# Strassen's algorithm for the up-projection of two chunks at a time, with weight sums kept in DRAM

## The chip, the cores and the metric

The kernel runs on one core of one Trainium2 chip. The metric is the device time of one execution in microseconds. A core has five engines that run side by side, each through its own queue in order: TensorE (PE in the profile, with its weight loads as PEld), VectorE (DVE), ScalarE (ACT), GpSimd (POOL), and SyncE (SP), which here only issues DMAs. PSUM, where matmuls accumulate, has eight banks of 512 float32 per partition.

## The reference

Sliding-window attention (8 batches, 8 heads, 576 positions, head dimension 64) is followed by a feed-forward part over all 4608 tokens:

```python
    scores = scale * np.matmul(q, k.transpose(0, 1, 3, 2))
    mask = (rel >= 0) & (rel < window)          # window = 128
    scores = np.where(mask, scores + bias[None], -1000000000.0)
    ...
    attn = attn / (np.sum(attn, axis=-1, keepdims=True) + 1e-09)
    return np.matmul(attn, v).astype(np.float32)
...
    h = x @ w_in                                # x 4608 x 512, w_in 512 x 2048
    g = h * (1.0 / (1.0 + np.exp(-1.702 * h)))
    return (g @ w_out).astype(np.float32)       # w_out 2048 x 512
```

x is the attention's output with the heads side by side. All data are float32.

## The kernel before

**Precision.** TensorE multiplies in a rounded 32-bit type (fp32r). Each operand is therefore kept as a high part, its rounded copy, and a low part, the difference; a product is three matmuls: high by high, low by high, high by low. The high part is a cast or copy on ACT or DVE, the low part a subtraction on POOL or DVE.

**Feed-forward.** The tokens are 18 chunks of T = 256; the 2048 hidden columns are 16 blocks f of 128 columns. For one chunk and one f, `Job.up` (L548) multiplies x (transposed, four blocks k of 128 rows) by the block of w_in: 12 matmuls of 128x256 (L552) into one PSUM tile `h_ps`. GELU is Tanh on ACT (L557) and one DVE operation (L558); `gh` (L561, ACT) and `gl` (L562, POOL) are its parts. `Job.down` (L565) multiplies them by the block of w_out: three terms by two row blocks, 6 matmuls of 512 columns (L571) into `acc0` and `acc1`, which stay open over all 16 f. A factor of two in GELU is taken out at the end (L587), and the result is sent from ACT's queue. `split_x` (L532) makes the parts of a chunk's x when the chunk begins. The two weights are decoded once into SBUF tiles `w1_0` to `w1_15` and `w2_0` to `w2_15`, each with both parts, and stay there.

**Attention.** It is software-pipelined: one `tick` (L609) takes one unit one step further. The first two batches are 24 units of another kind, all done early; each of the other six batches is 20 units (120 in all), of two blocks of 128 queries, or one at the end of a head pair. A unit's steps are: loads from SP's queue (`load`, `load_v`, kept in program order by `move`), splits, scores on PE (L334, PSUM tile `s_ps`, one bank), bias and row minimum on DVE (L362), Exp on ACT (L381), division on DVE, transposes on PE (L442, PSUM tile `t_ps`, two banks), high part on ACT (L455), low part on DVE (L461), product with V on PE (L499, `x_ps`), and sums into the chunk's x (`xf`, four buffers). PSUM's eight banks are `s_ps` 1, `t_ps` 2, `x_ps` 1, `h_ps` 2, `acc0`, `acc1`.

**Order.** The program goes through steps (chunk, f). In each step it first lets as many ticks go as the batches' due times ask for (L701 to L710), then issues `up` of the next step, then `down` of this one:

```python
        credit += pace
        while credit >= 1 and ticks < last:
            credit -= 1
            tick()
        ...
                j.up(nf)
        ...
        j.down(f)
```

A batch must be done two steps and a bit ahead of the first chunk that reads it (`SLACK`), and may start only when a chunk far enough along has begun (`start`, `seen`), since `xf` has four buffers. From chunk 2 on, one batch falls on two chunks, apart from chunk 6 and chunks 15 to 17, which have next to none.

This is not yet the order on the engines. The program is built with `schedule_with_timeline_sim=True`: a planner simulates the engines and gives each its queue, taking what is ready by its own times, the earlier in the program first. PSUM and SBUF tiles are handed out in the same simulation; a tile with a `tag` shares the buffers of that tag. `keep_in_program_order` and `in_turn` fix parts of the order. What the planner has ordered is carried out strictly, with semaphore waits.

Of the kernel before, what the change touches and what calls it, by code (L numbers as in the profile page):

```python
# [8 lines left out]
F32 = mybir.dt.float32  # L9
F32R = mybir.dt.float32r  # L10
# [3 lines left out]
AF = mybir.ActivationFunctionType  # L14
# [6 lines left out]
P = 128  # L21
# [23 lines left out]
SPINS = 10, 6, 6, 6, 6, 6, 6  # L45

# [96 lines left out]
def tile_kernel(ctx: ExitStack, tc: tile.TileContext, q0, k0, v0, qT, kT, v, w_in, w_out, out):  # L143
# [7 lines left out]
    ps = ctx.enter_context(tc.tile_pool(name="ps", bufs=1, space=PSUM))  # L151

# [276 lines left out]
    def flip(u):  # L429
# [4 lines left out]
        u.t = ps.tile([P, 4 * P], F32, name="t_ps", bufs=2)  # L434
# [28 lines left out]
    open_x = {}  # L463

# [67 lines left out]
    def split_x(c, x):  # L532
        xh = xp.tile([P, NC, T], F32R, name="xh")
        xl = xp.tile([P, NC, T], F32R, name="xl")
        for k in range(NC):
            (nc.scalar.copy if c in BESIDE else nc.vector.tensor_copy)(xh[:, k], x[:, k])
            sub = nc.vector if k % 2 else nc.gpsimd
            sub.tensor_tensor(xl[:, k], x[:, k], xh[:, k].bitcast(F32), ALU.subtract)
        return xh, xl

    class Job:


        def __init__(self, c, f0, f1, begun=None):
            self.c, self.f0, self.f1, self.begun = c, f0, f1, begun
            self.gs = {}

        def up(self, f):  # L548
            h = ps.tile([P, T], F32, name="h_ps", bufs=2)
            ops = [(z, x, k) for z, x in ((0, self.xh), (1, self.xh), (0, self.xl)) for k in range(NC)]  # L550
            for n, (z, x, k) in enumerate(ops):
                nc.tensor.matmul(  # L552
                    h, w1[f][:, z, k * P:(k + 1) * P], x[:, k],
                    start=(n == 0), stop=(n == len(ops) - 1))
# [20 lines left out]
        def finish(self):  # L575
# [6 lines left out]
            for t, acc in enumerate(self.acc):  # L582
# [6 lines left out]
                nc.scalar.dma_start(out[at:at + P, :], o[:, t])  # L589

# [81 lines left out]
    jobs += [Job(c, 0, NF) for c in range(2, NCH)]  # L672
    starts = {}
    steps = 0
    for j in jobs:
        starts.setdefault(j.c, steps)
        steps += j.f1 - j.f0
    now, credit, first_x = 0, 0.0, xf[0]
# [4 lines left out]
    def begin(j):  # L683
        j.xh, j.xl = split_x(j.c, xf.pop(j.c, first_x))
        j.up(j.f0)

    begin(jobs[0])
    seen = 0
    flat = [(j, f) for j in jobs for f in range(j.f0, j.f1)]
    for now, (j, f) in enumerate(flat):  # L690
# [10 lines left out]
        pace, last = 0.0, 0  # L701
        for n, by, start in due:
            if start > seen:
                break
            last = n + 3
            pace = max(pace, (n + 3 - ticks - credit) / max(starts[by] - 1 - SLACK - now, 1))
        credit += pace
        while credit >= 1 and ticks < last:
            credit -= 1
            tick()  # L710
# [7 lines left out]
        j.down(f)  # L718
        if f == j.f1 - 1:
            j.finish()  # L720
# [53 lines left out]
```

## Time and profile before

| | us |
|---|---|
| median of 3 runs | 1064.84 (1064.75 to 1067.0) |
| the profiled execution's own time | 1068.36 |
| its span, first to last instruction | 1066.3 |
| PE busy / weight loads | 1052.9 / 929.1 |
| DVE / ACT / POOL busy | 660.5 / 597.2 / 603.5 |
| DMA | 78.45 MB, 74 GB/s over the span |
| mean granted TensorE clock | 0.995 |

A matmul's busy time contains its way through the pipeline, so that neighbours overlap; starts of successive matmuls give the pace. In rows of instructions, the text is: line, engine, operation, output <- inputs, shape, count, then busy time and mean duration of one in ns, then idle time of the engine before them and what ended it. Rows with a time first are from the timeline: start, duration, engine, line.

### The profile page before, as it was taken

Reading aid. Unit: us, or ns where it says so; the run is one execution under the profiler, and the core shown is the slowest. Engines: PE = TensorE matmul, PEld = TensorE weight load, DVE = VectorE, ACT = ScalarE, POOL = GpSimd, SP = SyncE. Lnnn points to the kernel's source line nnn. Section 1 sums busy time; section 2 is a strip of 40 time slices with the busy share of each in tenths; the row PEclk is TensorE's granted clock in tenths of the full one; section 3 lists DMA queues with packets and bytes.
Section 4 is the critical chain, followed back from the end, with each engine's and each line's share of the span. In section 5 each row is a group of like instructions: output and inputs, shape, how many; then the busy total and the mean of one; then the engine's idle time right before and its main releaser. Section 6 shows DMA issues by size and latency. Waiting matters only on the chain.

```text
span 1066.3 us, 21362 instructions
## 1 busy us (share of the span) xinstructions
PE 1052.9 (99%) x7041; PEld 929.1 (87%) x7041; DVE 660.5 (62%) x2117; ACT 597.2 (56%) x1811; POOL 603.5 (57%) x863
## 2 busy tenths in 40 slices
PE   9899999999999999999999999999999999999998
PEld 5567787889989999999999999999999999998987
DVE  6797522568887777545767668767877687313121
ACT  6879853466666565535555556655665656322222
POOL 4579933567676666554656557656666665323232
PEclk9899999999999999999999999999999999999999
DMA  8872001223222132102121223212222221000000
GB/s 307 281 261 73 25 22 56 73 67 96 75 76 81 51 102 67 57 14 71 54 79 52 71 62 91 66 60 78 79 63 85 57 78 28 20 2 20 1 21 20
DMA packets 88109, 78.45 MB, mean 74 GB/s; under 512 B 36800, under 2 KB 79296, under 8 KB 88000
## 3 DMA queue, kind: packets, MB, share of 16 engines
q1 hardware_dynamic: 82240, 67.14, 21.4%
q10 hardware_dynamic: 5760, 9.96, 2.6%
q8 instruction: 55, 0.90, 0.3%
q14 instruction: 54, 0.44, 0.1%
HBM read 67.63 MB, written 9.44 MB: 72 GB/s over the span
## 4 chain that ended last, share of the span: by engine, by line
PE 94%; DVE 3%; ACT 1%; DMA 1%; issue 1%; POOL 0%; SPq 0%; DVEq 0%; POOLq 0%; ACTq 0%
PE h_ps L552 38%; PE acc L571 37%; PE s_ps L334 5%; PE x_ps L499 5%; PE t_ps L442 4%; PE x_ps L476 2%; PE t_ps L419 1%; PE sb_ps L324 1%; PE s_ps L324 1%; DVE wc L213 1%; DMA rw<-w_out 1%; ACT pb L374 1%; DVE rec L392 0%; PE acc L189 0%; DVE rw L212 0%
## 5 line engine op out<-in xcount | busy, mean ns | idle before, releaser
L562 POOL TENSOR_TENSOR gl<-g,gh 128x256 fp32r<-128x256 f32 x288 | 218.0, 757 | 292.2 <-ACT gh L561 224.9
L552 PE MATMUL h_ps<-xh,w 128*128 128x256 f32 x2304 | 370.2, 284 | 1.1 <-POOL w L217 0.6
L552 PEld LDWEIGHTS h_ps<-xh,w 128*128 128x128 f32 x2304 | 328.5, 189 | 34.5 <-issue 2.8
L571 PE MATMUL acc<-w,gh 128*128 128x512 f32 x1152 | 324.9, 400 | 0.0
L558 DVE SCALAR_TENSOR_TENSOR g<-g,h_ps 128x256 f32<-128x256 f32 x288 | 119.6, 415 | 207.9 <-ACT g L557 206.5
L557 ACT ACTIVATE g<-h_ps 128x256 f32<-128x256 f32 x288 | 110.4, 383 | 229.4 <-PE h_ps L552 207.3
L571 PEld LDWEIGHTS acc<-w,gh 128*128 128x128 f32 x1152 | 196.5, 189 | 27.9 <-ACT g L557 0.3
L552 PE MATMUL h_ps<-xl,w 128*128 128x256 f32 x1152 | 194.6, 280 | 0.0
L561 ACT CAST gh<-g 128x256 fp32r<-128x256 f32 x288 | 116.9, 406 | 129.5 <-DVE g L558 121.1
L571 PE MATMUL acc<-w,gl 128*128 128x512 f32 x576 | 188.0, 401 | 0.0
L552 PEld LDWEIGHTS h_ps<-xl,w 128*128 128x128 f32 x1152 | 164.2, 188 | 6.0
L312 POOL TENSOR_TENSOR K<-rk,K 128x384 fp32r<-128x384 f32 (+1 forms) x120 | 109.0, 909 | 65.2 <-ACT Q L292 15.9
L381 ACT ACTIVATE pb<-pb,mins 128x256 f32<-128x256 f32 (+2 forms) x216 | 104.9, 487 | 43.8 <-DVE mins L362 40.1
L571 PEld LDWEIGHTS acc<-w,gl 128*128 128x128 f32 x576 | 92.6, 188 | 9.5 <-issue 0.9
L311 POOL TENSOR_TENSOR Q<-rq,Q 64x256 fp32r<-64x256 f32 (+1 forms) x120 | 83.1, 692 | 22.2 <-DVE K L310 4.9
L406 DVE TENSOR_SCALAR pb<-pb,rec 128x256 f32<-128x256 f32 (+2 forms) x216 | 91.8, 461 | 3.2
L362 DVE CUSTOM_DVE_ANT_0 pb<-s_ps,bias 128x256 f32<-128x256 f32 (+3 forms) x240 | 85.7, 377 | 4.1 <-PE s_ps L334 2.8
L392 DVE TENSOR_SCALAR rec<-sums 128x2 f32<-128x2 f32 (+3 forms) x144 | 48.5, 336 | 58.4 <-ACT pb L381 53.6
L334 PE MATMUL s_ps<-K,Q 128*128 128x256 f32 (+1 forms) x432 | 79.8, 289 | 0.4 <-DVE mins L362 0.4
L310 DVE CAST K<-rk 128x384 fp32r<-128x384 f32 (+1 forms) x120 | 52.5, 438 | 41.2 <-PE s_ps L334 34.2
L461 DVE TENSOR_TENSOR pl<-t_ps,ph 128x512 fp32r<-128x512 f32 (+2 forms) x120 | 72.2, 604 | 9.3 <-ACT ph L455 6.6
L442 PE MATMUL t_ps<-ident,pb 128*128 128x128 f32 x408 | 74.2, 272 | 0.0
(68 smaller groups left out, 1322.2 us busy)
## 6 DMA issues: line engine op xcount, KB each, us to landing
rk<-kT SPq DMA_DIRECT2D x72, 192.0 KB, 2.5
rq<-qT SPq DMA_DIRECT2D x96, 128.0 KB, 2.3
out<-o ACTq DMA_DIRECT2D x36, 256.0 KB, 2.1
rw<-w_in SPq DMA_DIRECT2D x16, 512.0 KB, 6.5
rw<-w_out SPq DMA_DIRECT2D x16, 512.0 KB, 7.0
rk<-kT SPq DMA_DIRECT2D x48, 128.0 KB, 2.2
rv<-v SPq DMA_DIRECT2D x96, 64.0 KB, 1.9
rq<-q SPq DMA_DIRECT2D x16, 128.0 KB, 2.6
```

The source lines that it names most:

```text
L312: nc.gpsimd.tensor_tensor(K2, rk, K1.bitcast(F32), ALU.subtract)
L334: nc.tensor.matmul(u.s[:b.rows, e, b.first:b.end], u.Q[:, b.q0 - u.q0:b.q0 - u.q0 + b.rows], k[:, ko:ko + b.end - b.first], start=(z == 0) ...
L362: nc.vector.tensor_tensor_reduce(b.p[ra:rb, cs:b.end], u.s[ra:rb, e, cs:b.end], bias[head][ra:rb, cs:b.end], -SCALE, BIG, ALU.add, ALU.min ...
L381: nc.scalar.activation(live, live, AF.Exp, bias=u.mins[:b.rows, e:e + 1], scale=-1.0, accum_out=u.sums[:b.rows, e:e + 1],)
L406: nc.vector.tensor_scalar(live, live, u.rec[:rows, e:e + 1], None, ALU.mult)
L442: nc.tensor.transpose(u.t[:c.n, w:w + b.rows], b.p[:b.rows, col:col + c.n], ident[:b.rows, :b.rows])
L552: nc.tensor.matmul(h, w1[f][:, z, k * P:(k + 1) * P], x[:, k], start=(n == 0), stop=(n == len(ops) - 1))
L557: nc.scalar.activation(g, h, AF.Tanh, scale=0.851)
L558: nc.vector.scalar_tensor_tensor(g, g, 1.0, h, ALU.add, ALU.mult)
L561: nc.scalar.copy(gh, g)
L562: nc.gpsimd.tensor_tensor(gl, g, gh.bitcast(F32), ALU.subtract)
L571: nc.tensor.matmul(acc, g[:, t * P:(t + 1) * P], w2[f][:, z], start=(f == self.f0 and n == 0), stop=(f == self.f1 - 1 and n == 2))
```

## The change

Chunks 0 to 3 stay as they are. From chunk 4 on (`S0`) two chunks and two blocks f are one step of a 2 x 2 block product: the halves of the 512 rows of w_in are the block rows, the two f the block columns, and the two chunks the columns of x. Strassen's algorithm in Winograd's form makes the four results from seven block products instead of eight. Each product is 6 matmuls of 128x256 (two k, three terms). The results come together in two PSUM tiles, X and Y: products are added to X while copies of its state between them go to SBUF, and DVE adds Y. Two of the four results are read by GELU from SBUF, in a tile of 512 columns for both chunks.

- **Weight sums** (`sums`): from step 33 (chunk 2) to chunk 4, for each pair of f, POOL and DVE form four sums of blocks, ACT and POOL split them, and they and three plain blocks are written to DRAM from SP's queue, seven factors of 256 KB for each of eight pairs of f.
- **Ring** (`factor`): the factors come back two at a time, 512 KB, from SP's queue, into a ring of five tiles, in the place of `w1_7` to `w1_11`; a tile is asked for four tiles ahead.
- **Operands** (`Pair.split`): the seven sums of x are formed in place and split into seven tiles in the place of `w1_0` to `w1_6`, one buffer each.
- **GELU's parts** (`keep`): four tiles in the place of `w1_12` to `w1_15`.
- **Down-projection**: four accumulators for the two chunks, in `acc0`, `acc1` and the two banks of `h_ps`; it runs one pair of f behind, in quarters of six matmuls between the products.
- **PSUM of the attention**: X and Y take the two banks of `t_ps`; the transposes share the one bank of `s_ps`.
- **Due times**: a batch is due by the first chunk of the pair that reads it; the steps of a pair are 32 quarters.

```diff
+S0 = 4
+T2 = 2 * T
+RING = 5
+SUMS_FROM = 33
+ORDER = "A11", "A12", "S2", "S3", "S1", "S4", "A22"
+OPERANDS = "B11", "B21", "T2", "T3", "T1", "B22", "T4"
...
+    dram = ctx.enter_context(tc.tile_pool(name="dram", bufs=1, space=bass.MemoryType.DRAM))
...
-        u.t = ps.tile([P, 4 * P], F32, name="t_ps", bufs=2)
+        u.t = ps.tile([P, 4 * P], F32, name="t_ps", tag="s_ps" if paired else "t_ps", bufs=1 if paired else 2)
...
+    def sums(j):
+        f, g = w1[2 * j], w1[2 * j + 1]
+        H = 2 * P
+        for name, src in (("A11", f[:, :, :H]), ("A12", f[:, :, H:]), ("A22", g[:, :, H:])):
+            nc.sync.dma_start(part(j, name), src.bitcast(F32))
+        a = ffn.tile([P, 2 * H], F32, name="sa", tag="o", bufs=3)
+        b = ffn.tile([P, 2 * H], F32, name="sb", tag="o", bufs=3)
+        nc.gpsimd.tensor_tensor(a, g[:, 0].bitcast(F32), g[:, 1].bitcast(F32), ALU.add)
+        nc.gpsimd.tensor_tensor(b, f[:, 0].bitcast(F32), f[:, 1].bitcast(F32), ALU.add)
+        nc.vector.tensor_tensor(a[:, H:], a[:, :H], a[:, H:], ALU.add)
...
+        for s, names in ((a, ("S3", "S1")), (b, ("S2", "S4"))):
+            st = xp.tile([P, 2, 2 * H], F32R, name="st", tag="x0")
+            nc.scalar.copy(st[:, 0], s)
+            nc.gpsimd.tensor_tensor(st[:, 1], s, st[:, 0].bitcast(F32), ALU.subtract)
+            for i, name in enumerate(names):
+                nc.sync.dma_start(part(j, name), st[:, :, i * H:(i + 1) * H].bitcast(F32))
...
+    def factor(n):
+        tile_, side = divmod(n, 2)
+        while len(ring) < min(tile_ + RING, (NCH - S0) // 2 * len(parts)):
+            r = const.tile([P, 2, 2, 2 * P], F32R, name="ring", tag=f"w1_{len(OPERANDS) + len(ring) % RING}")
+            nc.sync.dma_start(r.bitcast(F32), parts[len(ring) % len(parts)])
+            ring.append(r)
+        return ring[tile_][:, side]
...
+            def cut(name, src):
+                i = OPERANDS.index(name)
+                t = self.x[name] = const.tile([P, 2, 2, T], F32R, name="x" + name, tag=f"w1_{i}")
+                nc.scalar.copy(t[:, 0], src)
+                on = nc.vector if i % 2 else nc.gpsimd
+                on.tensor_tensor(t[:, 1], src, t[:, 0].bitcast(F32), ALU.subtract)
+            cut("B11", a1)
+            cut("B21", a2)
+            nc.vector.tensor_tensor(a1, b1, a1, ALU.subtract)
+            cut("B22", b2)
+            nc.vector.tensor_tensor(b1, b2, b1, ALU.subtract)
+            nc.vector.tensor_tensor(b2, b2, a1, ALU.subtract)
+            cut("T2", b2)
+            cut("T3", b1)
+            cut("T1", a1)
+            nc.vector.tensor_tensor(a2, a2, b2, ALU.subtract)
+            cut("T4", a2)
...
+        def up(self, j, q):
+            if q == 0:
+                self.X = ps.tile([P, T], F32, name="X_ps", tag="t_ps", bufs=2)
+                self.product(j, 0, self.X, True)
+                self.p = ffn.tile([P, T], F32, name="p", tag="g")
+                nc.scalar.copy(self.p, self.X)
+                self.Y = ps.tile([P, T], F32, name="Y_ps", tag="t_ps", bufs=2)
+                self.product(j, 1, self.Y, True)
+                nc.vector.tensor_tensor(self.p, self.Y, self.p, ALU.add)
+                self.g = xp.tile([P, T2], F32, name="g1", tag="xh1")
+                self.gelu(self.g[:, :T], self.p)
+            elif q == 1:
+                self.product(j, 2, self.X, False)
+                self.u = xp.tile([P, T2], F32, name="u", tag="xh0")
+                nc.scalar.copy(self.u[:, :T], self.X)
+            elif q == 2:
+                self.product(j, 3, self.Y, True)
+                self.product(j, 4, self.X, False)
+                nc.scalar.copy(self.u[:, T:], self.X)
+                nc.vector.tensor_tensor(self.u[:, T:], self.Y, self.u[:, T:], ALU.add)
+            else:
+                self.product(j, 5, self.X, False)
+                self.gelu(self.g[:, T:], self.X)
+                self.keep(2 * j, self.g)
+                self.product(j, 6, self.Y, False)
+                nc.vector.tensor_tensor(self.u[:, :T], self.Y, self.u[:, :T], ALU.add)
+                g = xp.tile([P, T2], F32, name="g2", tag="xl0")
+                self.gelu(g, self.u)
+                self.keep(2 * j + 1, g)
+        def down(self, j, q):
+            if j == 0 and q == 0:
+                self.acc = [ps.tile([P, DM], F32, name="accs", tag=tag, bufs=bufs)
+                            for tag, bufs in (("acc0", 1), ("acc1", 1), ("h_ps", 2), ("h_ps", 2))]
+            f = 2 * j + q // 2
...
+        if now >= SUMS_FROM and made < NF // 2 and (now - SUMS_FROM) * NF // 2 >= made * (len(flat) - SUMS_FROM):
+            sums(made)
+            made += 1
...
+    paired = True
+    before = None
+    for c in range(S0, NCH, 2):
+        pair = Pair(c)
+        pair.split()
+        seen = c + 1
+        for i in range(NF // 2 * 4):
+            now += 1
+            advance(now)
+            pair.up(i // 4, i % 4)
...
+            elif i < 4:
+                before.down(NF // 2 - 1, i)
+            else:
+                pair.down(i // 4 - 1, i % 4)
+        before = pair
```

More of the change, by code (lines that the diff above doesn't have):

```diff
@@ L463, in tile_kernel @@
     open_x = {}
+    paired = False
     def mix_whole(u):
@@ L552, in up @@
                 nc.tensor.matmul(
-                    h, w1[f][:, z, k * P:(k + 1) * P], x[:, k],
+                    h, w1[f][:, z, k * P:(k + 1) * P], x[k],
                     start=(n == 0), stop=(n == len(ops) - 1))
@@ L671, in tile_kernel @@
     jobs.append(Job(0, F0, NF, jobs[0]))
-    jobs += [Job(c, 0, NF) for c in range(2, NCH)]
+    jobs += [Job(c, 0, NF) for c in range(2, S0)]
     starts = {}
@@ L677, in tile_kernel @@
         steps += j.f1 - j.f0
+    for c in range(S0, NCH):
+        starts[c] = steps + (c - S0) // 2 * 2 * NF
     now, credit, first_x = 0, 0.0, xf[0]
@@ L685, in begin, with advance @@
         j.up(j.f0)
+    def advance(now):
+        nonlocal credit
+        pace, last = 0.0, 0
+        for n, by, start in due:
+            if start > seen:
+                break
+            last = n + 3
+            pace = max(pace, (n + 3 - ticks - credit) / max(starts[by] - 1 - SLACK - now, 1))
+        credit += pace
+        while credit >= 1 and ticks < last:
+            credit -= 1
+            tick()
     begin(jobs[0])
-    seen = 0
+    seen, made = 0, 0
     flat = [(j, f) for j in jobs for f in range(j.f0, j.f1)]
@@ L699, in tile_kernel @@
                 decode_next()
[L701 to L710, printed above, removed]
+        advance(now)
+        if now >= SUMS_FROM and made < NF // 2 and (now - SUMS_FROM) * NF // 2 >= made * (len(flat) - SUMS_FROM):
+            sums(made)
+            made += 1
         if now + 1 < len(flat):
@@ L717, in tile_kernel @@
                 seen = max(seen, nj.c)
-        j.down(f)
-        if f == j.f1 - 1:
-            j.finish()
+            j.down(f)
+            if f == j.f1 - 1:
+                j.finish()
+    while made < NF // 2:
+        sums(made)
+        made += 1
+    paired = True
[6 more added lines that the diff above has]
+            now += 1
+            advance(now)
+            pair.up(i // 4, i % 4)
+            if before is None:
+                if i == 1:
+                    j.down(f)
+                    j.finish()
+                if i >= 4:
+                    pair.down(i // 4 - 1, i % 4)
+            elif i < 4:
+                before.down(NF // 2 - 1, i)
+            else:
+                pair.down(i // 4 - 1, i % 4)
+        before = pair
+    for q in range(4):
+        before.down(NF // 2 - 1, q)
 def build(nc, arrays):
```

62 lines of the change are left out of this document (58 added, 4 removed).

## The prediction

> **What bounds the kernel now.** I read the page first, then busy time by stretches of two chunks, then the order of the last matmuls.
>
> ```profile
> span 1066.3 us, 21362 instructions
> PE 1052.9 (99%) x7041; PEld 929.1 (87%) x7041; DVE 660.5 (62%) x2117; ACT 597.2 (56%) x1811; POOL 603.5 (57%) x863
> ...
> GB/s 307 281 261 73 25 22 56 73 67 96 75 76 81 51 102 67 57 14 71 54 79 52 71 62 91 66 60 78 79 63 85 57 78 28 20 2 20 1 21 20
> ```
>
> ```profile
> 0.00:45.00 45.00, 40.26 (x239) 25.47 (x239) 29.97 (x117) 31.85 (x99) 20.07 (x30) 0.93 0.81 274
> 90.00:130.00 40.00, 40.00 (x257) 31.07 (x257) 24.36 (x67) 38.95 (x113) 37.44 (x34) 1.00 0.15 42
> ...
> 186.10:307.30 121.20, 121.20 (x840) 108.75 (x839) 88.26 (x294) 76.62 (x244) 78.11 (x119) 1.00 0.28 78
> 307.30:424.10 116.80, 116.37 (x803) 106.93 (x803) 89.41 (x302) 70.71 (x219) 76.81 (x120) 1.00 0.27 75
> ...
> 581.60:697.10 115.50, 115.50 (x797) 106.55 (x796) 82.33 (x282) 68.36 (x209) 73.47 (x113) 1.00 0.25 70
> ...
> 923.70:1012.40 88.70, 88.70 (x574) 80.21 (x573) 21.28 (x48) 25.14 (x64) 26.75 (x36) 1.00 0.04 13
> ```
>
> The columns after the length are PE, PEld, DVE, ACT and POOL busy, granted clock, DMA share, GB/s. PE is never idle from chunk 2 (begun at 186.1) to the last chunk but for 0.4 us in one stretch; DVE is at most 77% busy (89.4 of 116.8). Two chunks beside a batch of attention take 115.5 us, two chunks alone 88.7 us. So the kernel is PE's queue, and a change is worth the matmuls that it takes out less the idle time that it makes. Busy time counts a matmul's pipeline, so the price of one is read from starts:
>
> ```profile
> 1054.62 1.09 PE L571 MATMUL acc<-w,gh 128*128 128x512 f32 x4
> 1055.55 0.28 PE L552 MATMUL h_ps<-xl,w 128*128 128x256 f32 x1
> 1055.67 0.63 PE L571 MATMUL acc<-w,gl 128*128 128x512 f32 x2
> 1056.14 1.10 PE L552 MATMUL h_ps<-xh,w 128*128 128x256 f32 x8
> 1057.08 0.62 PE L552 MATMUL h_ps<-xl,w 128*128 128x256 f32 x4
> 1057.54 1.09 PE L571 MATMUL acc<-w,gh 128*128 128x512 f32 x4
> 1058.47 0.63 PE L571 MATMUL acc<-w,gl 128*128 128x512 f32 x2
> 1058.94 1.09 PE L571 MATMUL acc<-w,gh 128*128 128x512 f32 x4
> ```
>
> Twelve up-matmuls of 256 columns go from 1056.14 to 1057.54, 116.7 ns each; six down-matmuls of 512 columns from 1057.54 to 1058.94, 233 ns each. Two chunks of 192 and 96 would be 89.6 us; the stretch shows 88.7. The single L552 at 1055.55, between two pieces of L571, shows that the planner mixes work of two steps.
>
> **What is removed.** Before, two chunks and two f take 4 groups of 12 up-matmuls, 48. After, seven products of 6 (two k, three high/low terms), 42, of the same 128x256 shape. Seven pairs of chunks by eight pairs of f by 6 is 336 matmuls, at 116.7 ns **39.2 us**. The down-projection keeps its 12 matmuls for each f and chunk pair (four row blocks, three terms), attention keeps all of its own. Nothing is added to PE. A pair falls to 115.5 − 5.6 = 109.9 us beside attention and to 83.1 us alone.
>
> **What is added beside PE.** The durations:
>
> ```profile
> L558 DVE SCALAR_TENSOR_TENSOR g<-g,h_ps 128x256 f32<-128x256 f32 x288 | 119.6, 415 | 207.9 <-ACT g L557 206.5
> L557 ACT ACTIVATE g<-h_ps 128x256 f32<-128x256 f32 x288 | 110.4, 383 | 229.4 <-PE h_ps L552 207.3
> L561 ACT CAST gh<-g 128x256 fp32r<-128x256 f32 x288 | 116.9, 406 | 129.5 <-DVE g L558 121.1 <-PE acc L571 5.6 <-DVE rec L393 1.4
> ...
> L217 POOL TENSOR_TENSOR w<-wc,w 128x512 fp32r<-128x512 f32 x32 | 45.9, 1442 | 6.6 <-ACT w L216 6.4
> ...
> L587 DVE TENSOR_SCALAR o<-acc 128x512 f32<-128x512 f32 x34 | 22.2, 684 | 6.0 <-PE acc L571 6.0
> ...
> L216 ACT CAST w<-wc 128x512 fp32r<-128x512 f32 x32 | 20.2, 630 | 4.8 <-DVE wc L213 4.6
> ...
> L584 DVE TENSOR_TENSOR o<-acc,xf 128x512 f32<-128x512 f32 x2 | 1.3, 686 | 0.4 <-DMA rv<-v 0.4
> ```
>
> ```profile
> L538 DVE TENSOR_TENSOR xl<-xf,xh x10: 412/928/958, 582.8 to 814.7; 128x256 fp32r<-128x256 f32 x10
> L538 POOL TENSOR_TENSOR xl<-xf,xh x10: 782/787/923, 583.1 to 813.1; 128x256 fp32r<-128x256 f32 x10
> ```
>
> DVE, for each pair of f: three adds and the GELU multiply that read PSUM, 4 × 0.415; one GELU multiply of 256 with both inputs in SBUF, not in the trace, bounded by the subtraction's 0.41 and 0.93 (minimum and median); one of 512, from 0.69 (L584) to 1.2 (0.93 plus the 0.27 by which 512 exceeds 256). That is 2.8 to 3.8 us, times eight 22 to 30. The split of x adds four additions and three subtractions of 512, 4.8 to 8.4, the finish two at 0.68. In all 28 to 40 us, where the stretch without attention has 21.3: **+7 to +19**, so 89 to 101 us of 109.9 beside attention.
> ACT: three copies at 0.41, two Tanh at 0.38, one of 512 at about 0.61 (0.383 + 0.630 − 0.406), two casts at 0.63: 3.9 × 8 = 31, split 7 × 0.63 = 4.4, finish about 1.2. 36.6 against 25.1; so 79.9 of 109.9.
> POOL: 16 + 4 subtractions of 512 at 1.44 = 28.8 against 26.8; so 75.5 of 109.9.
> Every engine stays under PE, so this work is hidden; without that cover DVE would set 101. For queueing behind a DVE at 81 to 92% I look at the nearest row, 77% busy with 0.4 us PE idle: 0.4 × 5 pairs = 2 at least, a us each = 5 at most, taken **3**.
>
> The Trainium skill, SBUF — State Buffer, section Who interferes with whom, says that a DVE instruction with two SBUF inputs and a GpSimd one that reads SBUF lock each other out for their whole length. The trace agrees as far as it goes: L538 on DVE takes 0.41 alone and mostly 0.93 beside its POOL sibling. By this rule the upper ends hold, 5 in place of 3; by the 0.41 alone, 2.
>
> **Sums of the weights**, once, between step 33 and chunk 4: eight times four POOL operations of 512, 46.1 us, on the 78.1 of the stretch from 186.1 to 307.3: 124.2 of 121.2, full. DVE gets 32 operations of 256 (13 to 30), ACT 16 × 0.63 = 10: 118 and 87 at most. A full POOL need not stop PE: from 90 to 130 POOL had 37.4 of 40 and PE no gap. What is late is gl, two matmuls behind every step. Lower bound 0, as the last sums may run on into a pair whose POOL is 69% busy; upper 8 (the 3 us overfull and 5 of late gl, an estimate); taken **3**. The 56 writes of 256 KB are 14.7 MB in 121 us, 121 GB/s on 78, where slices reached 307.
>
> **The ring.** 28 tiles of 512 KB for each pair, one every 3.0 us (3.9 beside attention), 177 GB/s alone or 134 + 70. Four are in flight or waiting: 11.9 (15.7) us of lead.
>
> ```profile
> rw<-w_in SPq DMA_DIRECT2D x16, 512.0 KB, 6.5
> ...
> SPq L155 <- POOL VV L300: 355.4, 80, 27.9
> ```
>
> The same size landed in 6.5 us while DMA moved over 260 GB/s, so 0 on the path; uncovered it is a rival below.
>
> **Seams between pairs** (six). Each operand tile of x is single: B22's is released by product 5 of the last f pair, and the second factor T2 waits behind it, since b2 is overwritten after B22 is cut. From that release: cast 0.63, DVE subtraction, b1 and b2 at 0.69 to 1.2 each, cast 0.63: 3.3 to 4.9 us, and 1.44 on POOL for its low part. PE has until then product 6, two products (0.7 each), two quarters of the down-projection (1.4 each): 4.9 us, 5.4 to the low part. Late by 0 to 0.9, and by up to 3.5 with the last f pair's DVE work ahead (four at 0.415, one at 0.69: 2.4 us); twelve more down-matmuls (2.8 us) can be drawn forward, as it does now at 1055.55. Taken 0.8, six times **5** (0 to 21). The first seam has operand tiles free since chunk 3's f = 6: **1** (0 to 3.5). The tail: after the last product add, Tanh, multiply and cast, 2.4 us, under 2.8 of down-matmuls, and then the low part 1.44: **1** (0 to 1.5).
>
> Sum, against the profiled execution of 1068.36: −39.2 + 3 + 3 + 5 + 1 + 1 = −26.2, 1042.2; the median of the runs lies 3.5 lower: **1039**. With no give-back 1025.6; with every upper bound (39) 1065.
>
> **Rivals.**
> *One PSUM bank for scores and transposes.* The transposes move from their two banks to the one of the scores, so the attention becomes a ring: scores, bias, transposes, cast, subtraction, next scores.
>
> ```profile
> 646.82 0.48 PE L334 MATMUL s_ps<-K,Q 128*128 128x256 f32 x2
> 649.42 0.42 DVE L362 CUSTOM_DVE_ANT_0 pb<-s_ps,bias 128x256 f32<-128x256 f32 x1
> ...
> 650.63 0.60 PE L442 MATMUL t_ps<-ident,pb 128*128 128x128 f32 x4
> 651.61 0.58 ACT L455 CAST ph<-t_ps 128x512 fp32r<-128x512 f32 x1
> 652.71 0.68 DVE L461 TENSOR_TENSOR pl<-t_ps,ph 128x512 fp32r<-128x512 f32 x1
> ```
>
> Bare it is 0.7 (two score matmuls take 0.48, two more 0.23) + 0.84 + 0.60 + 0.58 + 0.68 = 3.4 us before any hand-over. As it ran here, queues included, it is 3.0 (646.82 to 649.84) and 2.8 (650.63 to 653.39), 5.8 us. A batch is 20 units, so the window allows 109.9 / 20 = 5.5. For it: the example, and DVE gets fuller. Against: the waits here cost nothing and the order by program puts attention first; one unit in five has a single block. At 5.9 us a pair takes 118, 8.1 over, five pairs 40: **1079**. Slower (over 1067) from 5.8 us on. The Trainium skill, TensorE: Matmul & The Clock Gate, Part 1, says that an idle window of about 3.4 us halves the clock; the trace shows 0.93 where PE was idle 4.7 of 45 us. By it each such stall costs some 1.7 us more, 1087.
> *SP holds the ring.* A load of V stood at the head of SP for up to 27.9 us, waiting for POOL; ring loads behind it start that late. The slack is 15.7 − 6.5 = 9.2 us; one such hold costs 18.7: **1057**. Against: SP had nothing else to do then, so the wait may be plain idleness.
> *No gain.* The seams and sums cost their upper bounds: **1060 to 1066**.
>
> **How the numbers follow.** The forecast 0.55, with its own range 1027 to 1052; the bank 0.20; SP 0.12; no gain 0.13, of which 0.06 lies within 0.2% (2.1 us, about what can be told from no change) and hardly any above. So faster 0.74, same 0.06, slower 0.20. The range goes from the sum without give-back, 1025, to 1073, which leaves out the larger part of the bank's case.
>
> **What would show it.** PE matmuls 7041 − 336; 117 ns between up-matmuls as before; a pair alone about 84 us, beside attention 111; stretches of attention with PE idle under 1 us; no PE wait on a ring tile. PE gaps waiting for the subtraction from the transposes or for the bias prove the bank; gaps on ring DMA with SP waiting for POOL prove SP; gaps at the first products of a pair prove the seams. It is wrong if a pair alone doesn't fall by about 5 us, or if pairs beside attention don't.

## The result and the profile after

The changed kernel takes **1211.15 us** (median of 4 runs, 1208.09 to 1215.43) where the kernel before takes 1064.8 on the same chip: 1.1372 times as long, interval 1.1334 to 1.141. It is slower, 172 us above the forecast and far above the range, which ended at 1073. The page of the changed kernel, its totals and the slices of PE and its clock:

```profile
span 1206.3 us, 21363 instructions
PE 1099.8 (91%) x6705; PEld 936.6 (78%) x6705; DVE 810.9 (67%) x2212; ACT 669.1 (55%) x1890; POOL 660.2 (55%) x783
...
PE   9899999978869997999879997999789997999997
...
PEclk9899999988969997999969996999879996999999
```

336 matmuls are gone, 7041 to 6705, as predicted. Yet PE's busy time grew by 46.9 us, from 1052.9 to 1099.8, and its idle time inside the span from 13.4 to 106.5. Together that is the 140 us by which the span grew. The dips in the slices come in pairs: where PE falls to between 6 and 8, the clock mostly falls with it.

Why does busy time grow with fewer matmuls? The 336 were worth 39.2 us, so 86 are to be explained. PE was busy for 116.7 us while the clock stood at 0.50 (10.2 in the kernel before), so about 53 us, half of the difference, go with the clock. Most of the other 33 are probably the ends of matmuls that no longer overlap a neighbour: PE has 180 pauses in place of 14, and six matmuls that cost 0.70 us by their starts are busy for 0.88.

Busy time by stretches of the changed kernel (columns as before: length, PE, PEld, DVE, ACT and POOL busy, granted clock, DMA share, GB/s):

```profile
187.30:330.70 143.40, 129.31 (x822) 113.32 (x820) 112.08 (x301) 79.74 (x241) 110.27 (x143) 0.94 0.44 132
330.70:455.80 125.10, 111.60 (x696) 98.40 (x694) 95.91 (x274) 71.36 (x201) 74.78 (x92) 0.92 0.59 184
...
851.80:986.60 134.80, 122.07 (x741) 106.79 (x741) 101.37 (x293) 77.27 (x217) 74.84 (x96) 0.91 0.54 167
...
905.20:972.50 67.30, 65.45 (x429) 58.69 (x428) 48.80 (x143) 37.91 (x108) 34.75 (x45) 1.00 0.60 187
...
994.40:1012.70 18.30, 11.51 (x47) 8.63 (x47) 11.83 (x42) 8.56 (x22) 2.47 (x6) 0.63 0.09 31
1012.70:1023.20 10.50, 9.11 (x36) 7.74 (x36) 4.31 (x9) 4.05 (x9) 3.71 (x4) 0.50 0.36 119
1022.40:1091.60 69.20, 66.53 (x398) 57.70 (x397) 25.34 (x37) 20.94 (x49) 15.51 (x12) 0.99 0.49 160
```

Three things are to be seen. Chunks 2 and 3, with the sums of the weights, take 143.4 us where they took 119.8 (190.0 to 309.8, from first up-matmul to first up-matmul). A pair beside attention takes 125 to 135 us where 109.9 was predicted, yet five pairs of f in its middle (905.2 to 972.5) run with PE all but full. The loss lies in the first pair of f of each pair: from its first matmul to that of the second there are 29.5 to 40.6 us, while each of the others takes 12.7 to 15.1, about the eighth part of 109.9. And within that first pair of f there are 18 us (994.4 to 1012.7) in which next to nothing but attention runs, with PE at 11.5 us of work and the clock at 0.63. PE's longest sums of waits in the changed kernel (total, times, longest):

```profile
PE s_ps L341 <- DVE pl L468: 20.0, 23, 2.9
PE t_ps L449 <- DVE mins L369: 10.8, 17, 1.7
...
PE X_ps L679 <- ACT u L711: 6.7, 22, 0.7
```

The first is the scores of a unit behind the subtraction that reads the transposes of the unit before, the row that the prediction named as proof of the rival with one PSUM bank. PE's order at the end of a pair shows it (start, length, operation, idle time before and its releaser in brackets):

```profile
998.87 0.88 PE L341 MATMUL s_ps<-K,Q 128*128 128x256 f32 x4 [0.47 <-DVE pl L468]
...
1000.62 1.12 PE L449 MATMUL t_ps<-ident,pb 128*128 128x128 f32 x4 [0.23 <-DVE mins L369]
...
1003.80 0.77 PE L341 MATMUL s_ps<-K,Q 128*128 128x256 f32 x2 [0.56 <-DVE pl L468]
...
1012.73 2.05 PE L679 MATMUL Y_ps<-xT,ring 128*128 128x256 f32 x6
...
1017.57 1.65 PE L679 MATMUL X_ps<-xT,ring 128*128 128x256 f32 x6 [0.46 <-ACT u L707]
```

Scores, transposes, scores of the next unit, 4.9 us round (998.87 to 1003.80), with nothing on PE but the attention's own matmuls: the pair before is used up, and the next one has had its first two products (from 986.6) and waits for the rest of its x. Then its products go on at the halved clock, six matmuls in 1.65 to 2.05 us that take 0.88 at the full one. Without attention a pair of f takes 11.5 us, so eight take 92, where 83.1 were predicted.

The experiments follow by question. Every time is a median; ratios are against the kernel before on the same chip.

### The profile page after: what moved, and what is told of

The parts are those of the page before. It is cut to its first block, busy times and chain, and to the rows that moved or that the text cites. A ratio compares the mean times of both kernels' runs of the same rounds, so it can differ in the third digit from the quotient of the medians.

```text
span 1206.3 us, 21363 instructions
## 1 busy us (share of the span) xinstructions
PE 1099.8 (91%) x6705; PEld 936.6 (78%) x6705; DVE 810.9 (67%) x2212; ACT 669.1 (55%) x1890; POOL 660.2 (55%) x783
## 5 line engine op out<-in xcount | busy, mean ns | idle before, releaser
L732 PE MATMUL accs<-w,gs 128*128 128x512 f32 x1344 | 350.5, 395 | 1.8 <-ACT gs L689 1.8
L732 PEld LDWEIGHTS accs<-w,gs 128*128 128x128 f32 x1344 | 238.2, 189 | 41.3 <-ACT gs L689 2.8
L690 POOL TENSOR_TENSOR gs<-g,gs 128x512 fp32r<-128x512 f32 x112 | 155.7, 1391 | 154.7 <-PE Y_ps L679 75.9
L679 PE MATMUL X_ps<-xB,ring 128*128 128x256 f32 x672 | 107.0, 296 | 14.6 <-ACT u L711 6.7
L679 PE MATMUL X_ps<-xT,ring 128*128 128x256 f32 x672 | 111.3, 300 | 5.4 <-POOL xT L661 2.4
L679 PEld LDWEIGHTS X_ps<-xB,ring 128*128 128x128 f32 x672 | 89.7, 193 | 30.5 <-ACT u L711 15.3
L679 PEld LDWEIGHTS X_ps<-xT,ring 128*128 128x128 f32 x672 | 100.9, 204 | 14.6 <-POOL xT L661 3.3
L679 PE MATMUL Y_ps<-xT,ring 128*128 128x256 f32 x672 | 106.0, 294 | 5.5 <-DVE u L712 3.0
L679 PEld LDWEIGHTS Y_ps<-xT,ring 128*128 128x128 f32 x672 | 95.7, 199 | 11.5 <-DVE xT L661 4.0
L564 PE MATMUL h_ps<-xh,w 128*128 128x256 f32 x512 | 86.1, 295 | 2.0 <-DVE g L570 1.7
```

What stands on the lines that cost most here:

```text
L564: nc.tensor.matmul(h, w1[f][:, z, k * P:(k + 1) * P], x[k], start=(n == 0), stop=(n == len(ops) - 1))
L679: nc.tensor.matmul(bank, w[:, z, k * P:(k + 1) * P], x[:, y, k], start=start and i == 0, stop=i == len(ops) - 1, skip_group_check=True)
L690: nc.gpsimd.tensor_tensor(t[:, 1], g, t[:, 0].bitcast(F32), ALU.subtract)
L732: nc.tensor.matmul(self.acc[t], g[:, y, t * P:(t + 1) * P], w2[f][:, z], start=(f == 0 and n == 0), stop=(f == NF - 1 and n == 2))
```

## Experiments on the shared bank

**The kernel before with the change's bank for the transposes.** Nothing of Strassen's algorithm, no sums, no ring of weights.

```diff
-        u.t = ps.tile([P, 4 * P], F32, name="t_ps", bufs=2)
+        u.t = ps.tile([P, 4 * P], F32, name="t_ps", tag="s_ps" if paired else "t_ps", bufs=1 if paired else 2)
...
+                paired = paired or nj.c >= 4
```

> The kernel before, with one edit: from chunk 4 on the transposes share the one PSUM bank of the scores, as in the changed kernel; no Strassen, no sums, no ring. Theory ring (one bank lets only one unit of attention through per 6.5 to 7 us beside the feed-forward, where 5.8 us are to be had): the chunks that carry a batch grow by 15 to 25 us a batch, PE idles and its clock halves ahead of chunks 6, 9, 11, 13 and 15, in all 1130 to 1190 us. Theory seam (single operand tiles and crowded engines at the start of a pair make the loss, the bank does not matter): 1063 to 1070 us.

Measured: 1202.47 us, 1.1293 (1.1273 to 1.1312): 138.7 us more from this line alone, 12 above the range of theory ring and far from that of theory seam. Its page, one stretch of two chunks, and the group of the score matmuls, first in the kernel before and then here:

```profile
PE 1114.6 (93%) x7041; PEld 966.1 (80%) x7041; DVE 657.8 (55%) x2117; ACT 609.0 (51%) x1811; POOL 598.6 (50%) x863
```

```profile
550.70:686.10 135.40, 123.03 (x771) 109.52 (x770) 78.93 (x259) 64.11 (x189) 67.78 (x107) 0.90 0.20 55
```

```profile
L334 PE MATMUL s_ps<-K,Q 128*128 128x256 f32 (+1 forms) x432 | 79.8, 289 | 0.4 <-DVE mins L362 0.4
```

```profile
L334 PE MATMUL s_ps<-K,Q 128*128 128x256 f32 (+1 forms) x432 | 86.6, 323 | 37.8 <-DVE pl L461 34.9 <-POOL pb L367 2.2 <-DVE rec L393 0.7
```

Two chunks (8 and 9) take 135.4 us where they took 110.8 (531.4 to 642.2), about what the changed kernel takes. The idle time before the scores was 0.4 us in the kernel before and is 37.8 here. The same 7041 matmuls are busy for 1114.6 us instead of 1052.9, 61.7 more. Some 51 of them go with the clock, granted at 0.93 of full speed over the run: PE was busy for 111.8 us while it stood at 0.50, 10.2 in the kernel before, and about half of the difference is lost. Idle time grew from 13.4 to 86.9, 73.5 us. DVE is no busier than before (657.8 against 660.5), so a full DVE isn't needed for this loss; the bank is enough.

**The changed kernel with a bank of their own for the transposes.** They get the two buffers of `h_ps`; the third and fourth row blocks of the down-projection share one accumulator.

```diff
-        u.t = ps.tile([P, 4 * P], F32, name="t_ps", tag="s_ps" if paired else "t_ps", bufs=1 if paired else 2)
+        u.t = ps.tile([P, 4 * P], F32, name="t_ps", tag="h_ps" if paired else "t_ps", bufs=2)
...
-                            for tag, bufs in (("acc0", 1), ("acc1", 1), ("h_ps", 2), ("h_ps", 2))]
+                            for tag, bufs in (("acc0", 1), ("acc1", 1), ("h_ps", 2))]
+                self.acc.append(self.acc[2])
...
```

> The changed kernel, with the transposes in a bank of their own. To free it, the accumulators of row blocks 2 and 3 of a chunk pair are one (so the second chunk's output holds the sum of its two row blocks twice, and its own values are left out); every matmul, copy and DMA stays. Theory ring: the first pair of f of the five pairs beside attention falls from 34 to 41 us to about 15, the clock stays at 1.00 there, in all 1080 to 1120 us. Theory seam: within 15 us of 1211.

Measured: 1131.81 us, 1.0645 (1.0613 to 1.0676), 79.3 below the changed kernel, but 12 above the range of theory ring. One stretch of a pair beside attention:

```profile
581.70:697.10 115.40, 111.45 (x737) 100.24 (x737) 98.20 (x278) 74.43 (x210) 75.09 (x96) 1.00 0.63 200
```

In this pair the clock is back at 1.00. The five pairs beside attention take 130.8, 120.1, 115.4, 124.7 and 111.9 us, with the clock at 0.93 in the first and 0.96 in the fourth. So the bank costs 79 us in the changed kernel and 139 in the one before. They need not agree: with the bank mended, other losses of the change may come out that lay in its shadow, which is a reading that no run shows. A mended kernel doesn't follow from it: the buffers come from an accumulator that the computation needs, and a version with all accumulators and this bank wasn't tried.

## Experiments on the sums of the weights

**The kernel before with the sums in steps 33 to 63, written and never read.**

```diff
+SUMS_FROM, SUMS_TO = 33, 64
...
+    def sums(j):        # the change's own, with its tiles st, part and the writes
...
+        if SUMS_FROM <= now and made < NF // 2 and (now - SUMS_FROM) * NF // 2 >= made * (SUMS_TO - SUMS_FROM):
+            sums(made)
+            made += 1
```

> The kernel before, with the weight sums computed and written to DRAM in steps 33 to 63 as in the changed kernel, and never read. Theory sums (DVE and POOL are full there and the attention of batch 2 is late): the stretch of chunks 2 and 3 grows from 121 us to 135 to 145, in all 1078 to 1090 us. Rival (the late start of the first pair came from its own split, not from the sums): at most 1070 us.

Measured: 1101.89 us, 1.0353 (1.033 to 1.0375), 38 us for work priced at 3 (0 to 8), and above what either theory gave. Chunks 3 and 4 of the kernel before, and then of this one:

```profile
249.30:309.80 60.50, 60.50 (x428) 56.00 (x427) 51.36 (x172) 41.60 (x128) 43.11 (x68) 1.00 0.31 87
309.80:369.20 59.40, 58.97 (x405) 53.86 (x404) 45.35 (x154) 34.27 (x105) 38.69 (x60) 1.00 0.25 69
```

```profile
244.70:323.90 79.20, 69.58 (x442) 61.13 (x440) 68.93 (x201) 48.70 (x147) 67.63 (x88) 0.94 0.42 121
323.90:404.30 80.40, 71.55 (x432) 62.84 (x431) 58.15 (x191) 42.51 (x132) 52.00 (x76) 0.92 0.35 98
```

Each of the two chunks takes some 20 us more. No engine is full there: DVE and POOL have 68.9 and 67.6 of 79.2. PE's idle time in the two chunks grows from 0.4 to 18.5 us, and its busy time by 21.7, at a granted clock of 0.94 and 0.92 and with 41 more matmuls. What PE waits for there is DVE: 16.1 of 18.1 us of its waits, 6.0 of them for the division (L410), 3.6 for the subtraction that reads the transposes (L465), 2.1 for the row minimum. For `gl` on POOL it is 0.2.

**The same, spread over steps 33 to 223.**

```diff
-SUMS_FROM, SUMS_TO = 33, 64
+SUMS_FROM, SUMS_TO = 33, 224
```

> The kernel before with the sums made and written but never read, as in e3_sums (1101.9 us), the eight of them spread over steps 33 to 223 in place of 33 to 63. Theory crowding (each sum is hidden where the engines have room, and the 38 us of e3_sums come from eight in a row): 1064 to 1076 us. Rival (each sum costs PE its 5 us wherever it stands): 1095 to 1105.

Measured: 1083.15 us, 1.0174 (1.0158 to 1.019). Half of the loss is left, 19 us or 2.4 a sum, and this lies between the two expectations. Crowding is one part; another remains when the sums are spread.

**The first again, with its writes on POOL's queue instead of SP's.** SP's part of the wait view of the first (180 to 420 us) had shown why:

```profile
SPq L622 <- POOL st L620: 102.0, 13, 38.1
```

SP stood with a write at its head for up to 38.1 us, and attention's loads are behind it.

```diff
-            nc.sync.dma_start(part(j, name), src.bitcast(F32))
+            nc.gpsimd.dma_start(part(j, name), src.bitcast(F32))
...
-                nc.sync.dma_start(part(j, name), st[:, :, i * H:(i + 1) * H].bitcast(F32))
+                nc.gpsimd.dma_start(part(j, name), st[:, :, i * H:(i + 1) * H].bitcast(F32))
```

> e3_sums with one edit: the 56 writes of the sums go out from POOL's queue in place of SP's, so that the loads of the attention no longer stand behind a write that waits for POOL. Theory SP (the writes hold SP for up to 38 us in e3_sums, the loads come late and with them batch 2): 1066 to 1080 us. Rival (DVE and POOL are full there, the order of the loads does not matter): 1094 to 1110.

Measured: 1132.69 us, 1.064 (1.0612 to 1.0669), 31 us worse, which neither theory had. The likely reason is in the group of the writes: they are POOL's own work now, 0.73 us each, and with the 24 of the weights' parts (0.78 each) they add 42 us to it.

```profile
L622 POOL DMA_DIRECT2D part<-st x32 | 23.2, 727 | 0.3 <-POOL st L620 0.3
```

So this run can't judge SP's wait. The next does.

**The first without the 32 writes of the four sums.** The operations stay; what they make goes nowhere.

```diff
-                nc.sync.dma_start(part(j, name), st[:, :, i * H:(i + 1) * H].bitcast(F32))
+                pass
```

> e3_sums (1101.9 us) without the 32 writes of the four sums: they are computed and split by POOL, DVE and ACT as there, and the 24 plain blocks are still written, but nothing on SP waits for POOL's subtraction. Theory SP (loads of the attention stand behind those writes): 1066 to 1082 us. Theory engines (the operations themselves, in order on POOL and DVE, hold up the attention and the GELU): 1092 to 1105 us.

Measured: 1097.68 us, 1.0311 (1.0297 to 1.0325): 4 us less than with the writes, of 38. One stretch, chunk 3:

```profile
249.60:330.60 81.00, 69.75 (x445) 59.73 (x444) 73.39 (x207) 48.51 (x148) 66.63 (x88) 0.98 0.26 70
```

The chunk is no shorter than with the writes; what is saved lies in chunk 4, 68.4 us in place of 80.4, while chunk 2 is 3.8 longer. A wait of 102 us on SP was worth 4. The rest stays with the operations, and PE's waits in chunks 3 and 4 are again for DVE. That each of the sums' operations costs by where it stands in a queue, ahead of what PE waits for, fits this and isn't shown. The sums also take buffers that other tiles use (tags `o` and `x0`); no run tells that apart.

## Experiments on the pair itself

Without attention or sums a pair of f takes 11.5 us in the changed kernel (six in the 69.2 us from 1022.4) where the count of its matmuls gives 10.5 (42 of 256 columns and 24 of 512; a pair of chunks has eight pairs of f). PE's order there, with the copy on ACT that it waits for:

```profile
1053.88 0.88 PE L679 MATMUL X_ps<-xT,ring 128*128 128x256 f32 x6
1054.60 0.39 PE L732 MATMUL accs<-w,gs 128*128 128x512 f32 x1
1054.80 0.37 ACT L711 COPY u<-X_ps 128x256 f32<-128x256 f32 x1 [4.43 <-PE X_ps L679]
1055.22 0.98 PE L679 MATMUL X_ps<-xB,ring 128*128 128x256 f32 x6 [0.23 <-ACT u L711]
1056.04 0.88 PE L679 MATMUL Y_ps<-xT,ring 128*128 128x256 f32 x6
1057.13 0.98 PE L679 MATMUL X_ps<-xB,ring 128*128 128x256 f32 x6 [0.21 <-DVE g L685]
```

Products 4 and 5 follow each other into the same bank X with only one down-matmul between them, so PE waits until ACT has copied product 4; the matmuls that could fill the time were spent earlier. Two theories: the two banks X and Y are too few, or the order is wrong.

**Y in other banks for the last two pairs**, those of the scores and of x, which attention no longer needs there.

```diff
-                self.Y = ps.tile([P, T], F32, name="Y_ps", tag="t_ps", bufs=2)
+                self.Y = ps.tile([P, T], F32, name="Y_ps", tag="t_ps" if self.c < FREE else ("s_ps", "x_ps")[j % 2], bufs=2 if self.c < FREE else 1)
```

> The changed kernel, with Y of the last two pairs (chunks 14 to 17, no attention left) in the banks of the scores and of the product with V, by turns, so that X alone has the two banks of before. Theory chain by bank (a pair of f takes 11.5 us in place of 10.5 because the next X waits for the GELU that reads the last one): 10.5 to 11.0 us for each pair of f, in all 8 to 16 us less than the changed kernel, 1195 to 1203. Rival (the waits are those for the copies of X between products of one pair of f): 11.3 to 11.5 us as before, 1205 to 1215.

Measured: 1214.78 us, 1.1414 (1.1388 to 1.144), no gain on the changed kernel's 1.1372 (1.1334 to 1.141), as the rival had it. More banks for Y don't help.

**The program's own order for the products and down-matmuls of the last two pairs**, each chained to the one before.

```diff
-    ring = []
+    ring, last_pe = [], []
...
+        def inline(self, m):
+            if self.c >= FREE:
+                if last_pe:
+                    in_turn([last_pe[0], m])
+                last_pe[:] = [m]
...
```

> The changed kernel, with the products and the down-matmuls of the last two pairs (chunks 14 to 17) kept on PE in the order of the program, so that six down-matmuls stand between the product that a copy of X waits for and the next one. Theory copies (11.5 us in place of 10.5 for a pair of f because the planner spends the down-matmuls early and leaves X's copy and GELU uncovered): 10.5 to 10.7 us for each of the 16 pairs of f, in all 10 to 16 us less than the changed kernel, 1194 to 1202. Rival (the time is lost to the rate of the ring or to DVE): 11.3 to 11.6, 1207 to 1215.

Measured: 1195.54 us, 1.1233 (1.1214 to 1.1252), 15.6 below the changed kernel, from two pairs, as theory copies had it. PE's order in it, and the stretch of six pairs of f:

```profile
1063.06 0.88 PE L686 MATMUL X_ps<-xB,ring 128*128 128x256 f32 x6
1063.77 0.88 PE L686 MATMUL Y_ps<-xT,ring 128*128 128x256 f32 x6
1064.49 1.55 PE L739 MATMUL accs<-w,gs 128*128 128x512 f32 x6
1065.88 0.88 PE L686 MATMUL X_ps<-xB,ring 128*128 128x256 f32 x6
```

```profile
1023.50:1087.00 63.50, 63.46 (x397) 57.30 (x397) 25.72 (x37) 22.92 (x50) 15.82 (x13) 1.00 0.55 178
```

PE has no gap: six down-matmuls, 1.4 us, stand now between products that use one bank. 63.5 / 6 is 10.6 us a pair of f, 0.9 less than 11.5, and 16 pairs of f make 14 of the 15.6 us.

**Own bank and program order for all seven pairs**, the second experiment with this one; two row blocks again share an accumulator.

```diff
-FREE = 14
+FREE = 4
...
+                            for tag, bufs in (("acc0", 1), ("acc1", 1), ("h_ps", 2))]
+                self.acc.append(self.acc[2])
...
```

> e2_own_bank (1131.8 us) with the products and down-matmuls of all seven pairs kept on PE in program order, as e6_pe_order did for the last two. Row blocks 2 and 3 share an accumulator as there, so the second chunk of a pair gets their sum in place of its own values. Theory chain (the copies and the GELU of X leave gaps in the pairs beside attention too): 15 us from the last two pairs and 10 to 25 from the others, 1092 to 1107 us. Theory DVE (beside attention DVE sets the pace, the order of PE does not help there): only the last two pairs gain, 1114 to 1120.

Measured: 1099.68 us, 1.0319 (1.03 to 1.0337), 32 below the own bank alone. Its first two pairs and six pairs of f without attention:

```profile
332.90:467.40 134.50, 118.61 (x762) 105.57 (x761) 119.72 (x356) 87.86 (x251) 87.12 (x112) 0.94 0.59 182
467.40:581.10 113.70, 109.42 (x734) 99.17 (x734) 93.25 (x276) 75.18 (x211) 74.19 (x96) 1.00 0.65 205
...
927.00:990.40 63.40, 63.40 (x398) 57.19 (x397) 24.86 (x37) 22.64 (x50) 15.62 (x13) 1.00 0.57 189
```

With both repairs the pairs beside attention after the first take 113.7, 113.8, 113.9 and 106.9 us, and one without is all PE. What is left above the kernel before is the way to the first pair (332.9 where chunk 4 began at 309.8, 23.1 us) and the first pair itself, 134.5 where two chunks took 117.3 (309.8 to 427.1). Its DVE has 356 operations where the second has 276: the last sums and the split fall into it. The six pairs behind it take 629.7 us to the end of the span, only 9.5 less than the same chunks before (427.1 to 1066.3), where their 288 matmuls less are worth 33.6.

**Own bank without the division of the probabilities on DVE.**

```diff
-            nc.vector.tensor_scalar(live, live, u.rec[:rows, e:e + 1], None, ALU.mult)
+            if not paired:
+                nc.vector.tensor_scalar(live, live, u.rec[:rows, e:e + 1], None, ALU.mult)
```

> e2_own_bank (1131.8 us) without DVE's division by the row sums in the batches that run beside pairs (the attention's output is left unnormalised there; row blocks 2 and 3 share an accumulator as in e2_own_bank): some 23 us of DVE work less for each of five batches, everything else stays. Theory DVE (pairs beside attention take 112 to 125 us in place of 109.9 because DVE is 84 to 88% busy and each operation stands in its queue): 6 to 12 us less a pair, 1075 to 1102 us. Theory chain (X's copies make the gaps, DVE has room): 1122 to 1135.

Measured: 1123.26 us, 1.0538 (1.0518 to 1.0558), 8.5 below the own bank alone. A lighter DVE helps a little, as theory chain had it. The order gave 32, but about half of that comes from the last two pairs (15.6 in the changed kernel), where there is no division; beside attention it is some 16 against 8.5.

## A version with what was learned

**Strassen's algorithm for chunks 14 to 17 alone**, where attention has ended and the bank is free, with the program's order, and the sums spread over steps 33 to 189.

```diff
-S0 = 4
+S0 = 14
+FREE = 14
+SUMS_TO = 190
...
```

Two more edits follow from it: the last batch may start one chunk earlier, and the outputs from chunk 12 on go through other buffers.

> A version: Strassen for chunks 14 to 17 alone, where no attention is left; PE order of those pairs as in e6_pe_order; the sums spread over steps 33 to 190; the transposes keep their banks all the time; the last batch may start one chunk earlier, with chunk 17's x in the place of x0. By the matmul count 2 x 5.6 us less than before, with 2 to 6 us given back for sums, seams and the first f pair: 1056 to 1061 us. If the sums cost 38 us wherever they stand: about 1092. If a pair of f stays at 11.5 us: about 1070.

Measured: 1086.63 us, 1.0211 (1.0186 to 1.0236), outside all three of the expectations. Its first pair:

```profile
902.40:989.00 86.60, 83.72 (x524) 74.83 (x523) 42.89 (x68) 35.19 (x76) 25.74 (x22) 1.00 0.53 171
```

The first pair takes 86.6 us where two chunks without attention took 89.7 (925.3 to 1015.0). From the last pair's first product to the end there are 96.1 us, as many as the last two chunks took before (970.2 to 1066.3), so the algorithm pays some 3 of the 11.2 us that the count gives: it gives some back in its first pair of f (12.6 us in place of 10.6) and behind its last product (12.2 us to the end, where 8.8 follow the last up-matmul of the kernel before). The whole is 22.5 us longer than before. The chunks ahead of the first pair, where the sums are made, take 713.2 us (189.2 to 902.4) where they took 681.2, with PE idle for 15.8 us in place of 0.5. Some 9 of these 32 us are attention that the kernel before did in chunk 14.

**The same with the sums at eight steps chosen for light load.**

```diff
+SUMS_AT = 25, 28, 31, 97, 100, 103, 106, 109
...
+        if made < NF // 2 and now >= SUMS_AT[made]:
```

> c14_last_two_pairs (1086.6 us) with the eight sums at steps 25, 28 and 31 (second part of chunk 0, before batch 2 may start) and 97 to 109 (chunk 6, next to no attention) in place of every 20 steps from 33 to 190. Theory crowding (a sum costs PE about 2 us only where attention fills DVE and POOL): 1064 to 1074 us. Theory engines (a sum costs its 2 us wherever it stands): 1083 to 1090.

Measured: 1083.38 us, 1.0179 (1.0165 to 1.0193), 3 us better, with intervals that overlap, and as theory engines had it. Where the sums stand matters little once they are spread, and no version here beats the kernel before.

## Why the prediction was wrong, step by step

**What failed is the choice among the rivals.** "One PSUM bank for scores and transposes" was named, with its row, and given a chance of 0.20. It happened, and it alone, put into the kernel before, costs 138.7 us. Its price, 1079, failed too, in two places.

*The length of the loop.* The prediction took 5.9 us a unit (its rows add up to 5.8) against an allowance of 5.5, from an example in which two banks let one unit's steps overlap the next one's. In the first experiment 20 units took from 310 to 455 us, 7.2 each: the first twelve, beside the feed-forward, 8.8 each and the last eight 5.0. Beside a pair of the changed kernel it is 7.4 (890.5 to 994.0, 14 units). One loop in the changed kernel:

```profile
904.82 0.56 PE L341 MATMUL s_ps<-K,Q 128*128 128x128 f32 x3
...
909.28 0.46 ACT L462 CAST ph<-t_ps 128x384 fp32r<-128x384 f32 x1
...
911.88 0.54 DVE L468 TENSOR_TENSOR pl<-t_ps,ph 128x384 fp32r<-128x384 f32 x1
...
914.64 0.63 PE L341 MATMUL s_ps<-K,Q 128*128 128x256 f32 x4
...
919.55 0.64 PE L341 MATMUL s_ps<-K,Q 128*128 128x256 f32 x4
```

The cast ends at 909.74, the subtraction starts 2.1 us later; it ends at 912.42, the next scores start 2.2 us later, behind matmuls that PE had taken first. This loop took 9.8 us, the next 4.9. With two banks such a wait delays its own unit; with one, by the program, every unit that follows. The bare 3.4 us and one undisturbed example were the wrong rows to price it by.

*What is late next.* At such a length, four or five of 20 units are left when a pair's products are spent. They run alone at 4.0 to 5.4 us each, with PE 63% busy in the stretch shown, and the clock is halved. The prediction charged only the overrun of the loop, 8.1 us a pair, and by the Trainium skill (TensorE: Matmul & The Clock Gate, Part 1) 1.7 for each stall. In the first experiment some 51 of the 138.7 us go with the lower clock. The Trainium skill, TensorE: Matmul & The Clock Gate, section A second HAM failure mode: psum-queue depth-cycling, says of another kernel that PE pausing briefly but often while it cycles through PSUM banks makes the clock swing between half and full. The trace agrees: the clock fell to 0.50 at 999.3, with no pause over 0.88 us in the 10 us before. The prediction had drawn on the first part of that page alone, where a long pause is needed.

**The term "sums" failed by its size**, 3 (0 to 8) against 38 alone and 21 to 23 us on the way to the first pair beside the change's own work. The working compared totals, POOL's 124 us with the stretch's 121, and took what is late to be `gl`. The trace shows something else: POOL was not full (67.6 of 79.2), PE hardly waited for `gl`, and 16.1 of 18.1 us of its waits were for DVE's part of the attention and of the feed-forward, while two chunks took 40 us more. The step that failed is the choice of what is late: `gl`, behind a POOL that may be full because "a full POOL need not stop PE", which was argued from a stretch in which POOL did other work. Of the 38 us, 19 vanish when the sums are spread and 4 with the writes on SP's queue; that the other 15 or so go with the operations is a remainder and not a measurement.

**DVE's durations** were at the upper bound or above it. In the changed kernel:

```profile
L413 DVE TENSOR_SCALAR pb<-pb,rec 128x256 f32<-128x256 f32 x139 | 77.0, 577 | 1.9
L685 DVE SCALAR_TENSOR_TENSOR g<-g,u 128x512 f32<-128x512 f32 x56 | 65.2, 1164 | 18.1 <-ACT g L684 18.0
L685 DVE SCALAR_TENSOR_TENSOR g<-g,p 128x256 f32<-128x256 f32 x56 | 56.8, 1015 | 12.2 <-ACT g L684 11.9
...
L685 DVE SCALAR_TENSOR_TENSOR g<-g,X_ps 128x256 f32<-128x256 f32 x56 | 23.4, 418 | 21.8 <-ACT g L684 21.0
```

The GELU multiply of 256 columns takes 418 ns with one input in PSUM and 1015 with both in SBUF, above the 0.93 taken as its end; that of 512 takes 1164. With the three adds at 0.42 that is 3.86 us a pair of f, 30.9 a pair, where the range ended at 30. DVE's load beside attention was right all the same, 89 to 101 predicted and 93 to 101 in the pairs shown but for the first, and **PE's queueing behind it**, priced 3 for five pairs, is at most 8.7 for the four pairs after the first in the kernel with both repairs (113.7, 113.8, 113.9 and 106.9 against 109.9), if nothing else is in that difference. A wrong size there, not a wrong sign.

**A step that was missing**: a pair of f without attention was taken at PE's count, 10.4. The planner's order left 11.5 (16 us in the last two pairs, by the experiment that fixes their order, and 32 with the own bank over seven). The prediction counted the down-matmuls as filling that could be drawn forward; drawn forward, they were missing where two products share a bank.

**What was right.** The count of matmuls and their price: in order, a pair of f takes 10.6 us, and a pair 85.2 from its first product to that of the next (83.1 predicted). The seams, 0.8 us: in order and without attention, the first pair of f behind the last seam takes 11.3 us, 0.7 more than the others. The ring: no wait of PE on a ring tile, 512 KB landed in 3.6 us; the rival with SP holding the ring fell, though SP did stand behind writes in the stage of the sums.

Taken from the changed kernel, the bank is worth 79.3 us and the order on top of it 32.1, and 35 above the kernel before stay. The effects measured singly come near the whole too: 1064.8 − 39.2 for the matmuls + 138.7 for the bank + 38.1 for the sums + 15.6 for the order is 1218.0, against 1211.15. That they do is in part luck, since the bank's own part in the changed kernel is only 79.

## What to carry to other kernels

When a change takes a buffer away from a pipeline, price the loop that it closes with the queue waits as they stand, each of them serial now, and then ask what runs alone at the end of the stage and what that does to the clock. That the totals fit doesn't make work beside a full engine free: look at which waiting instruction each added one stands ahead of, and spread such work out. Filling work is worth something only where it stands when the gap comes, so fix its order.

## What the hardware showed that was not expected

The clock stayed halved after the load had come back: in the changed kernel from 1012.7 to 1023.2, PE had 9.11 of 10.5 us busy at 0.50, and in the next 10.5 us it was at 1.00. The traces of the two kernels and the twelve runs, behind their first 60 us, show how busy PE must be for that. Each spell at 0.50 lasts a multiple of 3.4 us. Each of 63 falls to 0.50 came behind a stretch of 3.4 us in which PE was busy for at most 64%, and no stretch below 53% left the clock full. Each of 69 returns came behind one of at least 86%, and none above 92% left it halved.

A DVE multiply with both inputs in SBUF is two or three times as long beside POOL. In the changed kernel (minimum, median and longest in ns):

```profile
L685 DVE SCALAR_TENSOR_TENSOR g<-g,p x56: 406/1226/1930, 342.5 to 1187.0; 128x256 f32<-128x256 f32 x56
...
L685 DVE SCALAR_TENSOR_TENSOR g<-g,X_ps x56: 405/421/423, 359.7 to 1194.4; 128x256 f32<-128x256 f32 x56
...
L685 DVE SCALAR_TENSOR_TENSOR g<-g,u x56: 667/992/1804, 365.6 to 1196.1; 128x512 f32<-128x512 f32 x56
```

Laid beside POOL's elementwise operations in the same trace, the 56 multiplies of 256 columns with both inputs in SBUF part cleanly: the 11 that met none took 406 to 427 ns, the 45 that met one 554 to 1930. Of 512 columns, the 7 that met none took 667 to 692, and 44 of the other 49 took longer. With one input in PSUM, 13 met one and none took over 423. The Trainium skill, SBUF — State Buffer, section Who interferes with whom, says that the two engines lock each other out when a DVE instruction with two SBUF inputs meets a POOL one that reads SBUF. The trace agrees, by these numbers; no run here changed POOL's share alone. The probabilities' division, with one tensor in SBUF, grew as well, from 433 ns in the kernel before to 577: of its 168 operations of 256 columns the 58 that met none of POOL's have a median of 348 ns and none over 439, the 110 that met one a median of 616 and up to 2004.

A DMA issued from POOL's queue took 727 ns of POOL's own time, in the run that moved the writes there.
